# Moving the final 2.5 KB store of a decode block, and the wait for it, from SyncE to ScalarE

## The chip, the cores and the metric

The kernel runs on one core of one Trainium2 chip. Times are device microseconds (us) of that core; each execution has a reported time and, from its records, a span: the time from the first to the last recorded instruction of the program. The reported time is 1.2 to 1.8 us longer than the span, and that remainder turns out to matter here. I call it the time outside the span. The record calls a run fast when it is within 1.5% of the fastest of its kernel; every run used for a comparison below is fast (the state of a single execution, sp_warm below, is unknown and is marked).

## The reference, cut to what matters

A decode step for two rows of 640: layer norm with a conditioning modulation, attention over a cache window of 1024 positions with 32 heads of 192, then a gated feed-forward. Only the last line matters for the change: the result is 2 x 1 x 640 bf16, 2.5 KB.

```python
mod = (_silu(c) @ w_mod).reshape(c.shape[0], 6, 1, -1)      # sa, ca, ga, sb, cb, gb
h = _layernorm(x, axis=-1) * (1 + ca) + sa
x = x + ga * _A_ref(h, A_k_cache, A_v_cache, A_wq, A_wo)    # attention
h = _layernorm(x, axis=-1) * (1 + cb) + sb
x = x + gb * _B_ref(h, B_w_gate, B_w_up, B_w_down)          # feed-forward
return x
```

## The kernel before

The kernel is written as a list of operations for each engine. A small scheduler turns reads and writes of named buffers into semaphore waits. SyncE ("sp") issues all the large loads; ScalarE ("act") issues two small ones at the start; all of them are recorded at one line, L287, that of the helper `k_dma`.

```python
def k_dma(dst, src):                                          # L287
    return lambda e: e.dma_start(dst, src)
# ... (start of the program)
S.dma("act", k_dma(crow[:, :], c[:, :]), sem_c, writes=["crow"], name="ld_c")
S.dma("act", k_dma(xr[0:P:RB, :], A_x[:, 0, :].rearrange("b (i n) -> i b n", i=NR)), sem_x, writes=["xr"], name="ld_x")
# ... (end of the program)
S.op("dve", lambda e: e.tensor_tensor(out=fin[:, :], in0=ps[:, BK_OT, CY:CY + DR], in1=modR[:, 5, :], op=ALU.mult),
     reads=[bank(BK_OT), ("modR", 1)], writes=["fin"], name="gb_y")
S.op("dve", lambda e: e.tensor_tensor(out=finb[:, :], in0=fin[:, :], in1=X[:, :], op=ALU.add),
     reads=["fin", "X"], writes=["finb"], name="outR")
S.dma("sp", k_dma(out[:, 0, :].rearrange("b (i n) -> i b n", i=NR), finb[0:P:RB, :]),
      sem_out, reads=["finb"], name="st_out")
# ... (each engine's list is written out; "tail" comes after its last operation)
S.emit("sp", nc.sync, tail=lambda e: e.wait_ge(sem_out, 16))
S.emit("pool", nc.gpsimd)
S.emit("act", nc.scalar)
S.emit("dve", nc.vector)
S.emit("pe", nc.tensor)
```

The result lies in SBUF in eight rows of 160 values, and the store writes them as 4 x 2 x 160 to DRAM.

Of the kernel before, what the change touches and what calls it, by code (L numbers as in the profile page):

```python
# [119 lines left out]
def bass_adaLN_cond__sliding_block_cached__geglu_ffn__decode_kernel(  # L120
# [14 lines left out]
    P = 128  # L135
# [7 lines left out]
    NR = 4  # L143
# [30 lines left out]
    RB = 16  # L174
# [10 lines left out]
    with es:  # L185
        S = _Sched(nc, es)
# [11 lines left out]
        for kind, b, t, z in tiles:  # L198
            j0, n = (K_SPLIT if kind == "k" else V_SPLIT)[b][t]
# [68 lines left out]
        finb = sb("finb", [P, DR], BF16)  # L268
# [15 lines left out]
        sem_out = S.sem("d_out")  # L284

        def k_dma(dst, src):
            return lambda e: e.dma_start(dst, src)  # L287
# [304 lines left out]
        for n, it in enumerate(tiles):  # L592
            kind, b, t = it
# [106 lines left out]
        for ci, (r0, nr) in enumerate(WD_SPLIT):  # L700
            def f(e, r0=r0, nr=nr):
# [10 lines left out]
             reads=[bank(BK_OT), ("modR", 1)], writes=["fin"], name="gb_y")  # L712
        S.op("dve", lambda e: e.tensor_tensor(out=finb[:, :], in0=fin[:, :], in1=X[:, :], op=ALU.add),
             reads=["fin", "X"], writes=["finb"], name="outR")
        S.dma("sp", k_dma(out[:, 0, :].rearrange("b (i n) -> i b n", i=NR), finb[0:P:RB, :]),
              sem_out, reads=["finb"], name="st_out")

        S.resolve()
# [6 lines left out]
        moved = body[n0:]  # L725
        del body[n0:]
        body[entry:entry] = moved
        S.emit("sp", nc.sync, tail=lambda e: e.wait_ge(sem_out, 16))
        S.emit("pool", nc.gpsimd)
        S.emit("act", nc.scalar)  # L730
        S.emit("dve", nc.vector)
        S.emit("pe", nc.tensor)
        held, size = {}, None
# [41 lines left out]
```

## Time and profile before

| | before |
|---|---|
| reported time, median of the first 3 runs | 185.97 us (185.91 to 186.12) |
| span of the profiled run | 184.9 us (reported 186.11) |
| share of DMA in the chain that ended last | 57% |
| ScalarE busy | 8% |
| result in SBUF until end of span | 1.78 us |

The last row is the difference of the trace's records in nanoseconds; the prediction gets 1.82 us for it from rounded figures. The page's lines, the end of the chain and the store's own rows are in the prediction below, where they are read. In a busy row of the page stand busy time in us, share of the span and number of instructions (PE is TensorE's matmuls, PEld its weight loads, DVE VectorE, ACT ScalarE, POOL GpSimd, SP SyncE; a q after the name means the engine's sequencer, which waits and issues). A row of a DMA queue has packets, MB and the share of the sixteen DMA engines' span. One view is only told there: the records of line L287, which give the length of each issue. Its columns are queue, operation and transfer, then duration in ns (shortest, median, longest), then the first and last start in us; the last column, shapes, is empty here. For the kernel before:

```profile
L287 ACTq DMA_DIRECT2D crow<-in_c_dram x1: 543/543/543, 0.8 to 0.8; - x1
...
L287 ACTq DMA_DIRECT2D xr<-in_A_x_dram x1: 606/606/606, 1.4 to 1.4; - x1
...
L287 SPq DMA_DIRECT2D out_dram<-finb x1: 694/694/694, 183.1 to 183.1; - x1
```

An issue here is the record in the row of the issuing engine's sequencer (SPq or ACTq). The movement of this store's data is not in it: the first data packet comes 1.294 us after the start of the issue of 0.694 us. The load of x has the store's pattern in the other direction, and the store's issue is the longest of the three.

### The profile page before, as it was taken

The numbers are of one execution on the slowest core, as the hardware profiler recorded it, in microseconds if no ns is written. First come the engines' busy times: TensorE is split into PE (matmuls) and PEld (weight loads), VectorE is DVE, ScalarE is ACT, GpSimd is POOL, SyncE is SP. The second block draws the span as 40 slices with busy tenths as digits, with TensorE's granted clock in tenths as the row PEclk, the third lists the DMA queues.
The fourth block names the chain that finished last, engine by engine and source line by source line (L and its number), as shares of the span: only waits on it lengthen the run. The fifth ranks groups of instructions, "written<-read, shape, count | busy, mean of one in ns | idle before, by whom it ended". The sixth has DMA issues, their size and how long they took to land.

```text
span 184.9 us, 1610 instructions
## 1 busy us (share of the span) xinstructions
PE 104.3 (56%) x843; PEld 26.1 (14%) x552; DVE 106.8 (58%) x97; ACT 14.5 (8%) x28; POOL 6.7 (4%) x29
## 2 busy tenths in 40 slices
PE   0015400937666096662598667748663299866853
PEld 0011000020000000001360002400000266411211
DVE  6213000039996489965994999387995649302311
ACT  2032100060000000001000000100000100220410
POOL 7700000000000000000000000000000000000000
PEclk9999999996999759998599999987999669999999
DMA  9999998999897999999898989899999989899980
GB/s 349 433 495 425 425 425 362 429 425 495 367 511 340 511 404 447 457 394 479 374 479 365 500 351 500 383 468 436 425 450 394 491 367 486 378 388 435 419 365 28
DMA packets 2626, 76.97 MB, mean 416 GB/s; under 512 B 314, under 2 KB 444, under 8 KB 572
## 3 DMA queue, kind: packets, MB, share of 16 engines
q1 hardware_dynamic: 2604, 76.88, 96.9%
q8 instruction: 5, 0.08, 0.2%
q14 instruction: 1, 0.01, 0.0%
q10 hardware_dynamic: 16, 0.01, 0.0%
HBM read 76.88 MB, written 0.00 MB: 416 GB/s over the span
## 4 chain that ended last, share of the span: by engine, by line
DMA 57%; DVE 22%; PE 17%; ACT 1%; issue 1%; SPq 0%
DMA arena<-in_A_k_cache_dram 36%; DMA arena<-in_B_w_down_dram 14%; DVE arena L518 12%; DMA arena<-in_w_mod_dram 8%; PE ps L581 8%; DVE S_sb L537 6%; PE ps L530 5%; DVE Em L567 2%; PE ps L470 2%; DVE negm L547 1%; ACT E_sb L555 1%; PE ps L558 1%; DVE M L543 0%; PE ps L551 0%; SPq L287 0%
## 5 line engine op out<-in xcount | busy, mean ns | idle before, releaser
L530 PE MATMUL ps<-arena,ident_b 128*128 128x512 bf16 x192 | 50.7, 411 | 30.2 <-DVE arena L518 30.1
L518 DVE TENSOR_TENSOR arena<-arena,qbc 128x3072 bf16<-128x3072 bf16 x32 | 54.8, 1749 | 11.1 <-DMA arena<-in_A_k_cache_dram 11.1
L581 PE MATMUL ps<-arena,Em 128*64 128x384 bf16 x256 | 24.5, 357 | 5.6 <-DVE Em L567 5.6
L537 DVE TENSOR_REDUCE S_sb<-ps 128x32 f32<-128x1024 f32 x16 | 19.5, 1219 | 8.4 <-PE ps L530 8.4
L581 PEld LDWEIGHTS ps<-arena,Em 128*64 128x64 bf16 x256 | 15.4, 121 | 29.8 <-DVE Em L567 22.2
L567 DVE TENSOR_TENSOR Em<-E_sb,maskE 128x2048 bf16<-128x2048 bf16 x8 | 18.0, 2282 | 2.6 <-PE ps L581 2.6
L492 PE MATMUL ps<-arena,hT 128*2 128x512 bf16 x60 | 4.7, 485 | 11.7 <-DMA arena<-in_A_wq_dram 11.7
L502 DVE CAST qrow<-ps 128x512 bf16<-128x512 f32 x1 | 0.7, 693 | 15.6 <-PE ps L492 15.6
L545 PEld LDWEIGHTS ps<-ident_f,M 128*1 128x1 f32 x2 | 0.2, 80 | 61.5 <-DVE M L543 61.5
L555 ACT ACTIVATE E_sb<-S_sb,nbias 128x256 bf16<-128x256 f32 x2 | 1.0, 507 | 69.3 <-DVE nbias L553 69.3
L651 DVE COPY arena<-ps 128x320 f32<-128x320 f32 x1 | 0.5, 491 | 10.1 <-PE ps L643 10.1
L643 PE MATMUL ps<-arena,oT 128*2 128x320 bf16 x96 | 3.9, 299 | 2.4 <-DMA arena<-in_A_wo_dram 2.4
L588 ACT ACTIVATE On<-ps,rden 128x384 bf16<-128x384 f32 x2 | 1.2, 582 | 47.5 <-PE ps L581 47.5
L403 PE MATMUL ps<-ident_b,crow 2*128 2x2 bf16 x5 | 0.4, 177 | 7.9 <-POOL zsel L383 7.9
L678 PE MATMUL ps<-arena,h2T 128*2 128x384 bf16 x40 | 3.8, 455 | 1.7 <-DMA arena<-in_B_w_up_dram 1.4
L470 PE MATMUL ps<-arena,scT 128*17 128x480 bf16 x40 | 4.3, 597 | 0.5 <-DMA arena<-in_w_mod_dram 0.5
L415 PE MATMUL ps<-Em,ident_b 128*128 128x512 bf16 x17 | 4.2, 379 | 0.2 <-issue 0.2
L408 DVE CAST X<-xr 128x160 f32<-128x160 bf16 x1 | 0.2, 244 | 6.1 <-DMA xr<-in_A_x_dram 6.1
L687 DVE TENSOR_TENSOR aR<-ps,gl 128x384 bf16<-128x384 f32 x1 | 0.6, 558 | 5.4 <-PE ps L678 5.4
L424 PE MATMUL ps<-st,selstat 128*128 128x2 f32 x4 | 0.9, 298 | 4.9 <-ACT sqj L420 4.9
L478 DVE TENSOR_SCALAR opc<-modR 128x160 f32<-128x160 f32 x2 | 0.5, 245 | 5.1 <-ACT modR L475 5.1
L492 PEld LDWEIGHTS ps<-arena,hT 128*2 128x2 bf16 x20 | 0.6, 100 | 15.8 <-issue 15.8
(89 smaller groups left out, 52.6 us busy)
## 6 DMA issues: line engine op xcount, KB each, us to landing
arena<-in_A_v_cache_dram SPq DMA_DIRECT2D x4, 6144.0 KB, 27.2
arena<-in_A_k_cache_dram SPq DMA_DIRECT2D x3, 6144.0 KB, 36.0
arena<-in_A_wq_dram SPq DMA_DIRECT2D x1, 7680.0 KB, 31.3
arena<-in_A_wo_dram SPq DMA_DIRECT2D x1, 6240.0 KB, 27.0
arena<-in_A_k_cache_dram SPq DMA_DIRECT2D x2, 3072.0 KB, 42.7
arena<-in_w_mod_dram SPq DMA_DIRECT2D x1, 4800.0 KB, 14.0
arena<-in_B_w_gate_dram SPq DMA_DIRECT2D x1, 1920.0 KB, 20.7
arena<-in_B_w_up_dram SPq DMA_DIRECT2D x1, 1920.0 KB, 22.7
```

The lines of the kernel that those rows point to most:

```text
L415: last = e.matmul(ps[:, BK_T, :], lhsT=ident_b[:, :], rhs=Em[:, 0, 0:512 // H, :].rearrange("p j h -> p (j h)"), start=True, stop=True)
L470: last = e.matmul(ps[32 * i:32 * i + RM, half, 0:MH].rearrange("p (m n) -> p m n", n=DR), lhsT=scT[:, k, :], rhs=wv[:, 3 * half:3 * half + ...
L492: last = e.matmul(ps[32 * i:32 * i + B, n, :], lhsT=hT[:, k, :], rhs=wv[:, kk, i, n * QW:(n + 1) * QW], start=(k == 0), stop=(k == KT - 1) ...
L518: S.op("dve", lambda e: e.tensor_tensor(out=kt, in0=kt, in1=qbc[:, b, :].unsqueeze(1).broadcast_to([P, JC, Dh]), op=ALU.mult), reads=[("qb ...
L530: last = e.matmul(o_ap, lhsT=ident_b[:, :], rhs=kt[:, :, t * GC:(t + 1) * GC], start=(t == 0), stop=(t == NCH - 1))
L537: S.op("dve", lambda e: e.tensor_reduce(out=S_sb[:, b, 2 * JC * pair:2 * JC * (pair + 1)], in_=ps[:, 2 * z:2 * z + 2, :].rearrange("p k (j ...
L547: S.op("dve", lambda e: e.tensor_reduce(out=negm[:, b, :].rearrange("p (h x) -> p h x", x=XQ), in_=ps[0:1, BK_T, 0:P].rearrange("p (h x) - ...
L555: S.op("act", lambda e: e.activation(out=E_sb[:, b, :], in_=S_sb[:, b, :], func=ACTF.Exp, scale=SCALE, bias=nbias[:, b:b + 1], accum_out=d ...
L567: S.op("dve", lambda e, z=z, j=j: e.tensor_tensor(out=Em[:, z, :, :], in0=E_sb[:, b, j:j + JE].unsqueeze(2).broadcast_to([P, JE, H]), in1= ...
L581: last = e.matmul(ps[64 * i:64 * i + 2 * H, BK_O, 0:ON], lhsT=Em[:, z, 2 * jp:2 * jp + 2, :].rearrange("p j h -> p (j h)"), rhs=view(it, l ...
L643: last = e.matmul(ps[32 * i:32 * i + B, bk, 0:w], lhsT=oT[:, t, :], rhs=wv[:, tl, lo:lo + w], start=(t < NR), stop=(t >= NT - NR), tile_po ...
L678: last = e.matmul(ps[32 * i:32 * i + B, bk, 0:FT].rearrange("p (m r) -> p m r", r=FR), lhsT=h2T[:, k, :], rhs=wk[:, i, :, :], start=(k == ...
```

## The change

Its intent is to take the last store off SyncE's list and put it, with the wait for it, at the end of ScalarE's. The whole diff:

```diff
-        S.dma("sp", k_dma(out[:, 0, :].rearrange("b (i n) -> i b n", i=NR), finb[0:P:RB, :]),
+        S.dma("act", k_dma(out[:, 0, :].rearrange("b (i n) -> i b n", i=NR), finb[0:P:RB, :]),
               sem_out, reads=["finb"], name="st_out")
...
-        S.emit("sp", nc.sync, tail=lambda e: e.wait_ge(sem_out, 16))
+        S.emit("sp", nc.sync)
         S.emit("pool", nc.gpsimd)
-        S.emit("act", nc.scalar)
+        S.emit("act", nc.scalar, tail=lambda e: e.wait_ge(sem_out, 16))
```

## The prediction

> **What bounds the kernel now.** I read the page first, for what the whole span is made of. The busy rows and the chain of waits are these:
>
> ```profile
> PE 104.3 (56%) x843; PEld 26.1 (14%) x552; DVE 106.8 (58%) x97; ACT 14.5 (8%) x28; POOL 6.7 (4%) x29
> ...
> q1 hardware_dynamic: 2604, 76.88, 96.9%
> ...
> q10 hardware_dynamic: 16, 0.01, 0.0%
> ...
> DMA 57%; DVE 22%; PE 17%; ACT 1%; issue 1%; SPq 0%
> ```
>
> The reader is to see two things. The kernel is a stream of loads with arithmetic beside it: queue q1, which SyncE feeds, fills 96.9% of the sixteen DMA engines' span, and DMA is 57% of the chain that ended last. And ScalarE, the engine that gets a new task, is busy for 8% of the span and is 1% of the chain. So the change can't reach the bound of the kernel through either engine's load. It can act only where the store itself lies, and I turn to the end of the chain of waits in order of time, where the columns are start, duration and what it was:
>
> ```profile
> 155.58 26.07 DMA arena<-in_B_w_down_dram
> 181.65 0.04 issue
> 181.70 0.39 PE ps L706 x12
> 182.08 0.01 issue
> 182.09 0.28 PE ps L706 x4
> 182.37 0.02 issue
> 182.39 0.34 DVE fin L711
> 182.73 0.02 issue
> 182.75 0.33 DVE finb L713
> ```
>
> The last weights land at 181.65 us, the last matmuls and two VectorE operations follow, and the result is in SBUF at 182.75 + 0.33 = 183.08 us. The chain as printed stops there; the span is 184.9 us. The missing 184.9 - 183.08 = 1.82 us is the store, which the timeline of the last microseconds and SyncE's own waits show:
>
> ```profile
> 183.10 0.69 SPq L287 DMA_DIRECT2D out_dram<-finb  x1
> ```
>
> ```profile
> SPq L287 <- DVE finb L713: 26.6, 1, 26.6
> ...
> SPq L728 <- DMA out_dram<-finb: 1.0, 1, 1.0
> ```
>
> SyncE has nothing else to do from its last load (issued at 156.1 us) on: it waits 26.6 us for the result, starts the store 0.02 us after it, takes 0.69 us to issue it, waits 1.0 us for it to land, and the span ends. So the tail is 0.02 + 0.69 + 1.0 = 1.71 us plus about 0.1 us of rounding and the final instruction. It lies wholly on the path that sets the end; nothing runs beside it.
>
> [...] 0.69 us of issue and then a separate 1.0 us until the semaphore. [...] ScalarE issues two loads at the start, on q10, by the same kind of instruction. [...]
>
> **The change part by part.**
> *Removed*: one issue from SyncE's list (0.69 us) and SyncE's final wait (1.0 us). The compared instruction orders show that this is all: SyncE has 16 rows where it had 17, ScalarE 24 where it had 23, and TensorE, VectorE and GpSimd have the same rows. No load moves, because the store was the last thing in SyncE's list.
>
> *Added*: the same issue and the same wait at the end of ScalarE's list. Is ScalarE free by then? The timeline of the end has its last work:
>
> ```profile
> 172.80 1.28 ACT L684 ACT_TABLE_LOAD   x1
> 176.06 0.49 ACT L684 ACTIVATE gl<-ps 128x384 f32<-128x384 f32 x1 [1.98 <-PE ps L678]
> ```
>
> It finishes at 176.06 + 0.49 = 176.55 us, 183.08 - 176.55 = 6.53 us before the result is there. It will stand at the semaphore as SyncE did, so this adds 0.00 us. Nothing of ScalarE's comes after the store in its list, so its wait blocks nobody.
>
> *The cost of the issue on ScalarE* is the one number that can differ. The line of the issuing helper gives, for ScalarE, 543 ns for the load of the condition vector (2 rows of 640) and 606 ns for the load of x, which has the store's very pattern the other way round (4 x 2 x 160 elements between eight SBUF rows and DRAM). For SyncE it gives 327 to 642 ns for the loads and 694 ns for the store. If ScalarE's load of x is the better model, the store's issue takes 606 ns, 0.09 us less; if a store costs more than a load on either engine, 694 ns, no difference; and the two ScalarE figures fell while SyncE was issuing as well (SyncE issued at 0.80, 1.19 and on, ScalarE at 0.80 and 1.39 us)[...]. I choose 0.65 us, the middle of 606 and 694: -0.04 us.
>
> *The movement*: 2 x 640 bf16 is 2.5 KB. q1 has been empty since 181.65 us (from then to the result the DMA share by stretches is 0.00), so the store waits behind nothing on q1 and would wait behind nothing on q10, which carried its only 16 packets at the start. Landing stays at 1.0 us: 0.00 us.
>
> *Moved off SyncE*: it now ends at about 156.5 us instead of 184.8. [...] I take 0.00.
>
> The sum: 0.00 + (-0.04) + 0.00 + 0.00 = -0.04 us on 185.97, so 185.93; I call it 185.9 us.
>
> **The rivals.**
> First, *a dearer issue or wake-up on ScalarE*: it [...]has not issued a DMA for 181 us. Against it: semaphore waits of ScalarE's compute end as promptly as others (pieces called issue of 0.02 us before ScalarE in the chain), and its two early issues cost no more than SyncE's. If the issue took twice 0.69 us, the time would be 185.97 + 0.7 = 186.7 us, still within 0.4%.
>
> Second, *SyncE was delaying the store*, by being held at other work or by its long queue, and ScalarE wins that back. Against it: SyncE started the store 0.02 us after the result and its queue was empty. There is nothing to win but part of 0.69 us: at best, with the 327 ns of its cheapest issue, 185.97 - 0.36 = 185.6 us.
>
> Third, *the end of the program*: the reported time is 186.11 us for the profiled run against a span of 184.9, so 1.2 us lie outside the profile. If that part depends on which engine arrives last, a few tenths could go either way, 185.7 to 186.3 us. Nothing in the profile speaks to it.
>
> Fourth, *ScalarE becomes the bound, or the store collides with its work*. The 6.53 us of slack speak against it; it would need ScalarE to be 6.53 us later than it was.
>
> **The range and the chances.** The whole tail is 1.82 us, 1.0% of the time: even if the store vanished it could not make the kernel 2% faster (3.7 us), and to make it 2% slower the tail would have to triple. The three runs before span 0.21 us, and the rivals put the time between 185.6 and 186.7, the low half likelier. I add some tenths for one set of runs against another: 185.5 to 186.5 us. The chances are 0.5% for faster, 99% for within 2%, 0.5% for slower.
>
> **What the profile would show.** If I am right: a row of ScalarE's queue for the store starts about 0.02 us after the end of the last VectorE operation and lasts 0.55 to 0.75 us; its wait for the store is about 1.0 us; SyncE's queue ends with the last load at about 156.5 us; the last 1.4 us of arithmetic before the store are the same; and packets move from q1 to q10. How many I estimate from the page: q10's 16 are 8 data rows of x and 2 of the condition vector[...]. So the store is 8 + 4 = 12 packets, and q1 goes from 2604 to 2592 and q10 from 16 to 28.
>
> Wrong would be shown by: an issue on ScalarE near 0.3 or above 1 us (the first two rivals), a landing unlike 1.0 us (queues differ after all), an unchanged span with a changed time (the third), or a change before 181 us, which I take to be impossible since no load moves; a difference there would be the run's, not the change's.

Marked cuts took out what no trace or run of this case shows: how an issue and the end of the program work, what an issue may wait for, and the reason for four of the store's twelve packets. The sum came to -0.04 us, so 185.93 us: -0.04 for the issue and 0.00 for the other three. The 0.00 of "Moved off SyncE" was an estimate of mine. The four packets can be read from the packet records: in the kernel before the store has eight packets of 320 bytes and four of 4 bytes, and q10's sixteen at the start are eight of 320, two of 1280 and six of 4.

## The result, and the profile after

The changed kernel took 186.04 us (median of 6 runs, 185.95 to 186.18), the kernel before 185.95 us (median of 6, 185.78 to 186.12). The ratio is 1.0005, with a 95% interval of 0.9992 to 1.0018: the same. A ratio here is the mean time of one kernel's fast runs over that of the other's of the same rounds, so it is not quite the ratio of the medians.

The page of the changed kernel, the lines that answer to those shown of before:

```profile
PE 106.7 (58%) x845; PEld 27.7 (15%) x552; DVE 106.7 (58%) x97; ACT 14.5 (8%) x28; POOL 6.7 (4%) x29
...
q1 hardware_dynamic: 2592, 76.87, 97.1%
...
q10 hardware_dynamic: 28, 0.01, 0.0%
...
DMA 56%; DVE 23%; PE 18%; ACT 1%; issue 1%; SPq 0%
```

Twelve packets moved from q1 (2604 before) to q10 (16 before). TensorE was busy for 106.7 us where it was 104.3, and SyncE's last load was issued at 157.2 us instead of 156.1. Both lie before anything that the change moved, and over the eleven traces of kernels that start alike, these two among them, TensorE's busy time lies between 104.3 and 108.2 us and the last load's issue between 155.3 and 157.2 us. The end of the chain in order of time (start, duration, what):

```profile
181.51 0.04 issue
181.55 0.66 PE ps L706 x16
182.22 0.02 issue
182.24 0.34 DVE fin L711
182.57 0.02 issue
182.60 0.32 DVE finb L713
```

The arithmetic after the last weights is as it was: 1.41 us from 181.51 to the result at 182.92, where before it was 1.43 us from 181.65 to 183.08. That the weights landed 0.14 us earlier is the run's own: no load was changed. The timeline and the record of the final wait:

```profile
175.87 0.49 ACT L684 ACTIVATE gl<-ps 128x384 f32<-128x384 f32 x1 [1.98 <-PE ps L678]
...
182.95 0.59 ACTq L287 DMA_DIRECT2D out_dram<-finb  x1
```

```profile
L730 ACTq EVENT_SEMAPHORE  x1: 17/17/17, 184.6 to 184.6; - x1
```

ScalarE's last compute ends at 176.36 us, it waits at the semaphore, starts the store 0.03 us after the result and issues it in 0.59 us, 0.10 us less than SyncE did. So the tail, from the result to the end of the span, got shorter, and yet the reported time did not. Taking each run's reported time minus its span shows where the rest is: 1.42 us on average for the changed kernel (6 runs, 1.36 to 1.46). The one run before whose span was known then gives 186.11 - 184.9 = 1.2 us. (Spans are listed to 0.1 us, so a single such difference is uncertain by 0.05 us.) About two tenths seemed to have moved to where the profile does not reach, and the first set of experiments was made for that.

### The profile page after: what moved, and what is told of

It is laid out like the page before. It is cut to its first block, busy times and chain, and to the rows that moved or that the text cites. A ratio compares the mean times of both kernels' runs of the same rounds, so it can differ in the third digit from the quotient of the medians.

```text
span 184.7 us, 1612 instructions
## 1 busy us (share of the span) xinstructions
PE 106.7 (58%) x845; PEld 27.7 (15%) x552; DVE 106.7 (58%) x97; ACT 14.5 (8%) x28; POOL 6.7 (4%) x29
## 3 DMA queue, kind: packets, MB, share of 16 engines
q1 hardware_dynamic: 2592, 76.87, 97.1%
## 4 chain that ended last, share of the span: by engine, by line
DMA 56%; DVE 23%; PE 18%; ACT 1%; issue 1%; SPq 0%
DMA arena<-in_A_k_cache_dram 35%; DMA arena<-in_B_w_down_dram 13%; DVE arena L518 12%; PE ps L581 9%; DMA arena<-in_w_mod_dram 8%; DVE S_sb L537 6%; PE ps L530 5%; DVE Em L567 2%; PE ps L470 2%; DVE negm L547 1%; ACT E_sb L555 1%; PE ps L558 1%; PE ps L551 1%; DVE M L543 0%; SPq L287 0%
## 5 line engine op out<-in xcount | busy, mean ns | idle before, releaser
L530 PE MATMUL ps<-arena,ident_b 128*128 128x512 bf16 x192 | 49.0, 398 | 29.0 <-DVE arena L518 29.0
L581 PE MATMUL ps<-arena,Em 128*64 128x384 bf16 x256 | 26.8, 381 | 5.6 <-DVE Em L567 5.6
L581 PEld LDWEIGHTS ps<-arena,Em 128*64 128x64 bf16 x256 | 16.5, 129 | 31.0 <-DVE Em L567 22.0
L492 PE MATMUL ps<-arena,hT 128*2 128x512 bf16 x60 | 5.8, 573 | 11.7 <-DMA arena<-in_A_wq_dram 11.7
```

The source lines that it names most:

```text
L492: last = e.matmul(ps[32 * i:32 * i + B, n, :], lhsT=hT[:, k, :], rhs=wv[:, kk, i, n * QW:(n + 1) * QW], start=(k == 0), stop=(k == KT - 1) ...
L530: last = e.matmul(o_ap, lhsT=ident_b[:, :], rhs=kt[:, :, t * GC:(t + 1) * GC], start=(t == 0), stop=(t == NCH - 1))
L581: last = e.matmul(ps[64 * i:64 * i + 2 * H, BK_O, 0:ON], lhsT=Em[:, z, 2 * jp:2 * jp + 2, :].rearrange("p j h -> p (j h)"), rhs=view(it, l ...
```

## The experiments

Two theories came first. Theory A: a shorter issue on ScalarE and a dearer end of the program, which depends on the engine that ends last, cancel each other. Theory B: all of it is noise. A third, theory C, was formed after the first set: SyncE's being parked early is what costs. Later a second question was added: why ScalarE's issue was shorter.

All the results in one table. The issue is the store's record. "First packet" is from the start of the issue to the store's first data packet and "tail" from the end of the last VectorE operation to the end of the span; both are differences of the trace's records in nanoseconds, for the profiled run. "Outside" is the mean of reported time minus span over the fast runs, whose spans are listed to 0.1 us. The row of the kernel before has its nine runs of the first set, and the trace shown above. The three sets of experiments ran on three chips, each with runs of the kernel before, to which its ratios refer (medians 185.98 to 186.03 us); the kernel before has 1.27 us outside in each of them. Issue, first packet and tail are from one trace each; the seven traces in which ScalarE stores after its early loads have issues of 0.586 to 0.602 us.

| run | issues | waits | issue, us | first packet, us | tail, us | outside, us (runs) | median, us | ratio |
|---|---|---|---|---|---|---|---|---|
| before | SyncE | SyncE | 0.694 | 1.294 | 1.778 | 1.27 (9) | 185.99 | 1 |
| changed | ScalarE | ScalarE | 0.592 | 1.234 | 1.730 | 1.42 (6) | 186.04 | 1.0005 |
| after_again | ScalarE | ScalarE | 0.591 | 1.230 | 1.727 | 1.41 (5) | 186.16 | 1.0007 |
| act_issue_sp_wait | ScalarE | SyncE | 0.590 | 1.229 | 1.727 | 1.24 (5) | 185.93 | 0.9994 |
| sp_issue_act_wait | SyncE | ScalarE | 0.683 | 1.279 | 1.775 | 1.45 (5) | 186.16 | 1.0010 |
| act_issue_pool_wait | ScalarE | GpSimd | 0.602 | 1.241 | 1.746 | 1.80 (5) | 186.37 | 1.0021 |
| act_issue_both_wait | ScalarE | both | 0.591 | 1.230 | 1.731 | 1.45 (4) | 186.16 | 1.0010 |
| act_issue_dve_wait | ScalarE | VectorE | 0.591 | 1.230 | 1.739 | 1.35 (4) | 186.00 | 1.0000 |
| act_issue_pe_wait | ScalarE | TensorE | 0.586 | 1.230 | 1.764 | 1.54 (4) | 186.31 | 1.0014 |
| sp_warm | SyncE | SyncE | 0.585 | 1.213 | 1.706 | 1.24 (1, state unknown) | 186.04 | none |
| act_cold | ScalarE | ScalarE | 1.103 | 1.264 | 1.759 | 1.40 (4) | 186.23 | 1.0021 |
| sp_xload | SyncE | SyncE | 0.634 | 1.266 | 1.753 | 1.26 (4) | 186.02 | 1.0004 |
| split_store | both | SyncE | 0.663 and 0.580 | 1.584 and 1.223 | 2.015 | 1.25 (4) | 186.26 | 1.0015 |

All kernels gave the right result.

### Who waits

**The changed kernel again** (no edit).

> The changed kernel once more, beside the others. Theory A (the two small terms cancel): the issue takes about 0.59 us as in the first trace, 0.10 less than SyncE's 0.69, but the time outside the profiled span (reported time minus span) is 1.4 us where the one run before that I can read had 1.2, so the ratio is 1.000 to 1.001. Theory B (noise alone): the difference between reported time and span is the same in both kernels once many runs are seen, 1.2 to 1.4, and the time is 0.1 us lower.

Measured: issue 0.591 us, ratio 1.0007. Outside the span 1.37 to 1.46 us in its five runs and 1.21 to 1.33 us in the nine runs of the kernel before on the same chip. The two sets do not overlap, so theory B falls for this term, though the total is within noise of no change.

**ScalarE issues, SyncE waits.**

```diff
-        S.emit("sp", nc.sync)
+        S.emit("sp", nc.sync, tail=lambda e: e.wait_ge(sem_out, 16))
...
-        S.emit("act", nc.scalar, tail=lambda e: e.wait_ge(sem_out, 16))
+        S.emit("act", nc.scalar)
```

> ScalarE issues the store, SyncE waits for it, as no engine of either kernel does alone. Theory A (the engine that arrives last sets the cost of the end of the program): the issue stays at 0.59 us and the time outside the span falls back to 1.2 us, so this beats both by 0.1 to 0.2 us, at 185.8. Theory B: time outside the span as in the changed kernel, and no difference to it beyond 0.1 us.

Measured: issue 0.590 us as in the changed kernel, 1.24 us outside as in the kernel before, 185.93 us. The waits of SyncE's queue (engine and line, what it waited for, us in total, times, longest) show the wait where the edit put it:

```profile
SPq L728 <- DMA out_dram<-finb: 28.6, 1, 28.6
```

The 28.6 us are harmless, since SyncE has nothing else to do. Theory A is confirmed in its issue and in its time outside the span. Against the changed kernel of the same set, which differs in the waiting engine alone, the median is 0.23 us lower (185.93 against 186.16 us; the five runs of each, 185.76 to 186.05 and 186.04 to 186.19, hardly overlap). Against the kernel before, the gain of 0.1 to 0.2 us did not show: it is the fastest by its median, but only 0.06 us below that of its set, and the ratio of 0.9994 (0.9982 to 1.0007) does not set it apart. Both terms together are 0.05 us of tail and 0.03 us outside, 0.04% of the time.

**The mirror: SyncE issues, ScalarE waits**, made from the kernel before by moving the tail alone to "act".

> The mirror: SyncE issues, ScalarE waits. Theory A: it has both small costs, the issue of 0.69 us and 1.4 us outside the span, and is the slowest of the four, 186.1 to 186.2. Theory B: 0.69 us of issue, outside the span as before, 185.95.

Measured: issue 0.683 us, 1.45 us outside, 186.16 us. So the time outside followed the waiting engine and not the issuing one: 1.41 us with ScalarE issuing and waiting, 1.24 with SyncE waiting for ScalarE's issue.

**ScalarE issues, GpSimd waits**, the tail moved to "pool".

> ScalarE issues, GpSimd waits. Theory A: the time outside the span depends on which engine ends last, so it may take a third value, between 1.1 and 1.6 us; issue 0.59 us. Theory B: like the other kernels, 1.2 to 1.4 us outside.

Measured: 1.80 us outside (1.77 to 1.83), a third value, above the 1.1 to 1.6 us that were expected, and the slowest by its median, 186.37 us, with a ratio whose interval excludes 1 (1.0008 to 1.0033).

**ScalarE issues, both ScalarE and SyncE wait**, the tail on both.

> ScalarE issues, and both ScalarE and SyncE wait for the store. So far the time outside the span was 1.24 to 1.27 us where SyncE waits, 1.41 to 1.45 where ScalarE does and 1.80 where GpSimd does. Theory A (each engine has its own cost of ending, and the dearest late one sets the end): 1.41 us outside as with ScalarE alone, because ScalarE is late here too; total 186.05 to 186.15. Theory C (it is SyncE's early end that costs, because it then stands parked at the end of the program since 157 us): 1.24 us outside, total 185.9.

Measured: 1.45 us outside (1.43 to 1.49). SyncE was as late as in the kernel before (its last record ends 4 ns before ScalarE's) and it did not help, so theory C falls: the cost (1.45 us against 1.24 when SyncE alone waits for ScalarE's issue) came with ScalarE's waiting to the end, not with SyncE's being early.

**VectorE waits, and TensorE waits**, the tail moved to "dve" and to "pe".

> ScalarE issues, VectorE waits. Theory A: VectorE has a cost of its own, not equal to 1.24, 1.41 or 1.80 except by chance[...]. Theory C: SyncE is parked early, so at least 1.41 us outside, whoever waits. The issue stays at 0.59 us.

> ScalarE issues, TensorE waits. Theory A: a fifth value of the time outside the span, perhaps below SyncE's 1.24, in which case it is the fastest so far. Theory C: at least 1.41 us.

Measured: 1.35 us outside for VectorE and 1.54 us for TensorE. So the order is SyncE 1.24 to 1.27, VectorE 1.35, ScalarE 1.40 to 1.45, TensorE 1.54, GpSimd 1.80; the hope that TensorE would be below SyncE did not hold. VectorE's value denies theory C once more, which asked for at least 1.41. What happens in that time can't be seen: no record of the program covers it. That it depends on the engine that holds the final wait, and so ends last, is shown; the mechanism is not. Ending last and having one more wait in the list went together in every run, and no run separates them.

### Why the issue was shorter on ScalarE

**An extra, identical store on SyncE about 3 us earlier**, of other data, overwritten by the real one.

```diff
+        S.dma("sp", k_dma(out[:, 0, :].rearrange("b (i n) -> i b n", i=NR), xr[0:P:RB, :]),
+              S.sem("d_warm"), reads=["xr", "aR"], writes=["out"], name="st_warm")
...
-              sem_out, reads=["finb"], name="st_out")
+              sem_out, reads=["finb"], writes=["out"], name="st_out")
```

> The kernel before, with an identical extra store (of other data, overwritten by the real one) that SyncE issues about 3 us before the real one, while it is still waiting for the result. Theory W (SyncE's 0.69 us is a first store's or a long sleeper's): the extra store takes 0.69 us and the real one about 0.59. Theory E (it belongs to SyncE issuing this pattern): both take 0.68 to 0.70 us. In both, the total stays within 0.2 us of the kernel before.

The records of line L287, as shown of before:

```profile
L287 SPq DMA_DIRECT2D out_dram<-xr x1: 695/695/695, 180.0 to 180.0; - x1
L287 SPq DMA_DIRECT2D out_dram<-finb x1: 585/585/585, 183.1 to 183.1; - x1
```

The same engine issues the same pattern twice, in 695 ns and then in 585 ns. So SyncE can issue this store as fast as ScalarE did, and what its sequencer did before is worth 0.11 us of issue. That is theory W. The total, 186.04 us in its one run, stayed within the expected 0.2 us. It leaves two readings: the first transfer of a kind is dear (F), or the long sleep is (L).

**The two small loads of the start moved to SyncE**, in the changed kernel (act_cold: the store is then ScalarE's first DMA) and in the kernel before (sp_xload: SyncE has then issued the pattern of x at the start).

```diff
... (pump gets the argument upto)
-        pump()
+        pump(upto=1)
...
-        S.dma("act", k_dma(crow[:, :], c[:, :]), ...
-        S.dma("act", k_dma(xr[0:P:RB, :], ...
+        S.dma("sp", k_dma(crow[:, :], c[:, :]), ...
+        S.dma("sp", k_dma(xr[0:P:RB, :], ...
+        pump()
```

Here `pump` issues the large loads, and the new argument holds it after the first.

> The changed kernel, but SyncE issues the two small loads of the start (right behind its first), so that the store is the first DMA that ScalarE issues. SyncE's warmed store took 585 ns and its first of that pattern 695, so what looked like a difference of engines may be one of history. Theory F (the first DMA of a kind on a sequencer is dear): ScalarE's store takes about 0.69 us. Theory L (a long sleep is dear: SyncE had slept 26 us, ScalarE 6.5): it stays at 0.59. SyncE's load of x, the same transfer that ScalarE made in 606 to 632 ns, should take as long within 0.1 us. Time outside the span 1.41 to 1.45 as ScalarE waits; total within 0.3 us of the changed kernel.

> The kernel before with the same two loads on SyncE, which then stores and waits as before. Theory F: the store on SyncE takes about 0.59 us, because SyncE has issued a load of that pattern at the start, although it still sleeps 26 us before. Theory L: 0.69. Time outside the span 1.24 to 1.27; total 185.9 to 186.0.

The records of line L287 of act_cold:

```profile
L287 SPq DMA_DIRECT2D crow<-in_c_dram x1: 317/317/317, 0.8 to 0.8; - x1
L287 SPq DMA_DIRECT2D xr<-in_A_x_dram x1: 670/670/670, 1.2 to 1.2; - x1
...
L287 ACTq DMA_DIRECT2D out_dram<-finb x1: 1103/1103/1103, 183.0 to 183.0; - x1
```

and of sp_xload:

```profile
L287 SPq DMA_DIRECT2D out_dram<-finb x1: 634/634/634, 183.3 to 183.3; - x1
```

Without its early loads ScalarE's issue takes 1.10 us, far above the 0.69 that theory F gave, while it slept no longer than in the changed kernel; that speaks against L. But SyncE's store after an early load of x takes 0.634 us, between the values of F and L. So in these traces, one for each edit, earlier DMAs of the same sequencer go with a shorter issue; neither theory has the sizes, and by how much an old one helps after 180 us is open. Nor are the two engines shown to be alike. With the same early loads behind them, SyncE's issue is 0.634 us and ScalarE's 0.592: history gave 0.06 of the 0.10 us between the kernels, and the other 0.04 us may be the engine or the longer sleep. With no such load behind it, SyncE took 0.694 us and ScalarE 1.10, but SyncE had issued the large loads.

Whether a first DMA as such is dear is open too. ScalarE's first one, the condition vector, takes 0.543 us at the start; SyncE, as its second, issues the same load in 0.317 us (0.311 in sp_xload). For x it is the other way, 0.670 us on SyncE against 0.606 on ScalarE, within the 0.1 us that was expected. ScalarE's two, at 0.80 and 1.39 us, fell while SyncE was issuing as well (at 0.80, 1.19 us and on).

The more useful finding is in the table. Against the changed kernel, act_cold's issue is 0.51 us longer, but its first packet comes 0.03 us later (1.264 against 1.234) and its tail is 0.03 us longer. In these runs the length of the issue did not add to the path in full: here 0.51 us of it were 0.03 us of tail, between the two kernels 0.10 were 0.05, and in sp_warm, against the kernel before, 0.11 were 0.07.

The totals of these two tell little. Act_cold has a ratio of 1.0021 (1.0003 to 1.0040), but one of its four runs took 186.80 us with a span of 185.4, and the others took 186.06 to 186.31. Both edits also change the start: the query weights are issued at 1.9 us where before it was 0.8, and TensorE waits for the condition vector, now behind the first large load in SyncE's queue, until 13.6 us, where it was 7.9 us in the kernel before and 6.5 in the changed one. What that does to the total was not followed.

**The store in two halves, one on SyncE and one on ScalarE at once**, SyncE waiting for both.

```diff
-        S.dma("sp", k_dma(out[:, 0, :].rearrange("b (i n) -> i b n", i=NR), finb[0:P:RB, :]),
-              sem_out, reads=["finb"], name="st_out")
+        sem_out2 = S.sem("d_out2")
+        for h, (q, sm) in enumerate((("sp", sem_out), ("act", sem_out2))):
+            S.dma(q, k_dma(out[:, 0, 2 * DR * h:2 * DR * (h + 1)].rearrange("b (i n) -> i b n", i=2), finb[64 * h:64 * (h + 1):RB, :]),
+                  sm, reads=["finb"], name="st_out%d" % h)
...
-        S.emit("sp", nc.sync, tail=lambda e: e.wait_ge(sem_out, 16))
+        S.emit("sp", nc.sync, tail=lambda e: (e.wait_ge(sem_out, 16), e.wait_ge(sem_out2, 16)))
```

> The store in two halves of 2 x 2 x 160, one issued by SyncE and one by ScalarE at the same moment, SyncE waiting for both. If the two issues run beside each other[...], the tail from the result to the end of the span falls from 1.78 to about 1.65 us, the time outside stays at 1.25, and the total is 0.1 us below the kernel before.[...]

The fall to 1.65 us was an estimate of mine.

The issues, and the GB/s moved in 40 equal slices of the window from 182.9 to 186 us, first of split_store:

```profile
L287 SPq DMA_DIRECT2D out_dram<-finb x1: 663/663/663, 182.9 to 182.9; - x1
L287 ACTq DMA_DIRECT2D out_dram<-finb x1: 580/580/580, 182.9 to 182.9; - x1
```

```profile
GB/s 0 0 0 0 0 0 0 0 0 0 0 0 0 0 0 0 17 0 0 0 4 12 0 0 0 0 0 0 0 0 0 0 0 0 0 0 0 0 0 0
```

and the same window of the changed kernel:

```profile
GB/s 0 0 0 0 0 0 0 0 0 0 0 0 0 0 0 0 21 13 0 0 0 0 0 0 0 0 0 0 0 0 0 0 0 0 0 0 0 0 0 0
```

The store's two lumps of data in split_store lie four to five slices of 0.0775 us apart. By the packet records ScalarE's half leaves 1.223 us after its issue starts and SyncE's 1.584 us after its own. The issues ran side by side (0.66 us from 182.93 us on, 0.58 us from 182.94), as the expectation's condition asks, and yet the total got longer, so the expectation misses: the second half's data left 0.36 us later, and the tail is 2.015 us where it was 1.778. That is a loss of 0.24 us, about the 0.28 us of the ratio (1.0015, 1.0000 to 1.0030). Why the second half left later is not shown: neither issue took longer than the whole store's on the same engine (0.694 and 0.592 us). Halving the store and doubling the queues bought nothing.

No version beats both kernels clear of noise.

## Why the prediction was right or wrong

The measured 186.04 us lies in the range and is the same as before within 2%, for the reason given: the whole matter is a tail of 1.8 us. By its steps:

- **Nothing else moves, and ScalarE is free.** Right. Its last compute ends 6.56 us before the result, and the predicted packet counts, 2592 and 28, are exactly those of the page. SyncE's queue ended at 157.6 us and not at 156.5, within what such runs differ by.
- **The issue, 0.65 us chosen between 0.606 and 0.694.** Measured 0.592 us, shorter than the choice. The prediction asked which engine issues and what the transfer is, and gave no term to what the sequencer had issued before (its first rival names it, only as a danger for ScalarE): with an identical store 3 us before it, SyncE takes 0.585 us, and with the two early loads behind it 0.634. So history gave a good half of the 0.10 us; the rest is open. Its argument that ScalarE's two early issues cost no more than SyncE's compared unlike transfers: the load of the condition vector takes 0.543 us on ScalarE and 0.317 on SyncE.
- **Landing stays at 1.0 us.** By the trace's records the wait from the end of the issue grew from 1.040 to 1.090 us. So the sum "issue plus landing" was the wrong model: 0.10 us less of the one gave 0.05 us more of the other, and act_cold shows that even 0.51 us of issue can pass almost unnoticed. The net of the two steps, -0.05 us, is close to the predicted -0.04, but that is luck: two errors, -0.06 in the issue and +0.05 in the landing, cancel.
- **Moved off SyncE, "I take 0.00".** This is the step that failed. It measured 1.42 - 1.27 = +0.15 us. Which engine arrives last was named as the third rival, whose few tenths hold the 0.15 us; in the sum it stood as nothing. The 0.00 was an estimate of mine that no trace showed: no record of the program covers the time outside the span.
- **The sum.** -0.05 + 0.15 = +0.10 us, which agrees with the medians (+0.09) and the ratio (1.0005, +0.09 us), where -0.04 was predicted. The ratio's interval includes 1, so the total alone does not show the sign; what is clear of noise is the term outside the span, whose runs do not overlap. The stated range has a slip: its upper end, 186.5 us, is below the 186.7 of its own first rival, though some tenths were to be added.
- **The rivals.** A dearer issue on ScalarE did not happen in the changed kernel, and would have cost little: act_cold has an issue of 1.10 us and a tail only 0.03 us longer, where the prediction would have added the whole 0.51 us. SyncE was not holding the store back: the start after the result was 27 ns before and 31 ns after. The third rival is the one that came true, at 0.15 us. ScalarE did not become the bound.

## What to carry to other kernels

When the last act of a kernel is a small store, first look at how long its whole tail is: here 1.8 us of 186 capped any gain below a per cent, whichever engine did it. Which engine waited last changed the time by up to 0.56 us here, outside what the profile shows (1.24 us with SyncE, the cheapest of the five, and 1.80 with GpSimd), so compare reported time minus span when two kernels differ by that little. Do not take it for granted that the length of a DMA's issue adds to the path (here 0.51 us of it were 0.03 us of tail): measure from the start of the issue to the landing.
